# Attention backward loop: the block-end statistics spread over GpSimd, VectorE and several units, with dK and dV taken in other units

## The chip, the cores and the metric

The kernel runs on one core of one Trainium2 chip. The metric is the device time of one launch in microseconds (us); several launches are taken and the median is given. Engines: PE is TensorE (PEld its weight loads), DVE is VectorE, ACT is ScalarE, POOL is GpSimd, SP is SyncE, which here issues the DMAs. Where runs of two kernels are compared, the ratio is the mean time of one kernel's runs over that of the other's of the same rounds, so it is not quite the ratio of the medians that stand beside it. The experiments ran on two chips of the same kind (e4, e6, e7 and e9 on one, the others on another, by the record); each was measured beside the kernel before on its own chip, so runs of different rounds are compared by their ratios.

## The reference, cut to what matters

The program computes a forward pass and all gradients of two attention blocks. Only block B's backward matters here: 16 query heads that share one key and one value head, sequence 2048, head size 28.

```python
q = (x @ wq).reshape(B, S, H, Dh)          # 16 heads
k = x @ wk;  v = x @ wv                    # one head each
scores = einsum("bhqd,bkd->bhqk", q, k) * Dh**-0.5
p = softmax(scores);  o = einsum("bhqk,bkd->bhqd", p, v)
...                                        # o @ wo, then jax.vjp for all gradients
```

The kernel recomputes p tile by tile. With e = exp(score), row sum l, D = sum(dO*o) and dS = p*(dP - D), it needs dV = p^T dO, dK = dS^T q, dQ = dS k. The kernel puts 1/l and D into the small operand: the tile `don` holds dO/l in its columns and D/l in column 0, so that dP - D, already divided by l, falls out of one matmul. Other names below: `dsT` is dS with keys on the partitions, `dsx` is dsT transposed on DVE for dK, `eN` is e transposed by a DMA for dV, `doT` is `don` transposed for dP, `onat` is the normalised o, and `qX` holds the queries that dK reads. The granted clock is the share of full speed at which TensorE was allowed to run.

## The kernel before

The loop walks through 64 blocks (256 queries x 2 heads) of eight units (256 keys each). It is software-pipelined: in the program's unit u, block b's exp is made for u = 8b to 8b+7, its statistics follow at 8b+9, its dP and dS 16 units after the exp, its dQ 18 units after it, its dK later still. So every unit holds work of several blocks. I call the units 0 to 7 by u mod 8. The order of the code is the order on each engine.

```python
for u in range(NU + 26):
    w = u - 16
    sp = two score banks (of three, shared);  dp = two dP banks (of two)
    rows_SD(u, sp, dp)                                   # PE: scores of u, dP of u-16
    nc.scalar.activation(out=et[..0..], in_=sp[0], func=Exp)              # ACT, L671
    nc.vector.tensor_tensor(out=dst[:, 0], in0=dp[0], in1=e.., op=mult)   # DVE, L676: dsT
    nc.scalar.activation(out=cp, in_=dp[1], func=Copy)                    # ACT, L678
    nc.gpsimd.tensor_tensor(out=dst[:, 1], in0=cp, in1=e.., op=mult)      # POOL, L679: dsT
    nc.scalar.activation(out=et[..1..], in_=sp[1], func=Exp)              # ACT, L681
    if u % 2 == 1: nc.sync.dma_start_transpose(en, et)   # SP: eN, for dV
    # [...]
    e = u - 9                                            # unit 1: the chain
    if e >= 0 and e % 8 == 0 and e // 8 < NB:
        onp = psS.tile(..., name="sps")                  # PE transposes of o into a score bank
        nc.vector.reciprocal(out=r_, in_=onp[..0:1])                      # L701
        nc.vector.tensor_tensor(out=onv, in0=onp, in1=r_, op=mult)        # L705: onat
        nc.vector.tensor_tensor(out=dn, in0=dnv, in1=r_, op=mult)         # L709: don
        nc.gpsimd.tensor_tensor(out=prod, in0=dnv, in1=onv, op=mult)      # L711
        nc.vector.tensor_reduce(out=Dq, in_=prod, op=add)                 # L713
        nc.vector.tensor_tensor(out=dn[..0:1], in0=Dq, in1=r_, op=mult)   # L714
    e = u - 13                                           # unit 5: don transposed, copied to doT
    x = u - 26                                           # dK: two groups of four matmuls in each unit
    # [...] all of them need dsx of the whole block
    # PE: o of u-1 and dQ of u-18, both into the bank oq
    # dV: in every second unit, from u = 8b + 14 on, one group of four matmuls; needs eN and don
    # unit 0: DVE copies o (oTs);  unit 1: ACT copies dQ (L774)
    nc.vector.transpose(out=dsx[b][:, tp], in_=dsT[u - 18])               # DVE, L780
```

## Time and profile before

1722.71 us, median of 3 runs (1716.72 to 1724.99). I took each unit's length from the trace as the time from the start of its first exp (L671) to that of the next unit, median over the blocks (here and in the later tables from block 4 on):

| unit | 0 | 1 | 2 | 3 | 4 | 5 | 6 | 7 | block |
|---|---|---|---|---|---|---|---|---|---|
| before, us | 1.46 | 2.02 | 4.51 | 2.11 | 1.74 | 1.51 | 1.46 | 1.52 | 15.68 |

Units 0 and 5 to 7 take about 1.5 us; units 1 to 4 take longer. (The unit medians add up to more than the block's 15.68, since the blocks differ: about every third takes 16.6 us.) From the page of the kernel before, the span in 40 slices: busy tenths of PE and ACT, and the granted clock of PE. The loop fills slices 14 to 37, the last of them in part.

```profile
PE   2786767992985988888888888888888988888398
ACT  0321200120449887787778778778778777875122
PEclk9996886995985598888888888888888888888699
```

No engine is full, and the clock is at eight tenths. The engine that the stall holds up shows in the list of waits (who waited for whom, us in total, times, longest):

```profile
ACT eT L671 <- PE dps L623: 174.5, 100, 2.9
DVE dsT L676 <- PE dps L623: 156.8, 265, 3.6
PE dk_acc L623 <- DVE dsx L780: 120.8, 64, 2.6
```

Once in each of 64 blocks PE waits for DVE's dsx, and ACT and DVE then wait for PE. The timeline of DVE through units 1 and 2 of one block (start us, length us, engine, line, what; in brackets idle time before it and what ended it) shows why dsx is late:

```profile
1008.67 0.64 DVE L676 TENSOR_TENSOR dsT<-dps,eT 128x512 bf16<-128x512 f32 x1
1009.24 0.16 DVE L701 RECIPROCAL rl<-sps 128x4 f32<-128x4 f32 x1
1009.43 0.29 DVE L705 TENSOR_TENSOR onat<-sps,rl 128x128 bf16<-128x128 f32 x1
1009.64 0.99 DVE L709 TENSOR_TENSOR don<-do_nat,rl 128x128 bf16<-128x128 bf16 x1
1010.95 0.29 DVE L713 TENSOR_REDUCE Dq<-prod 128x4 f32<-128x128 f32 x1 [0.32 <-POOL prod L711]
1011.27 0.18 DVE L714 TENSOR_TENSOR don<-Dq,rl 128x4 bf16<-128x4 f32 x1
1011.35 0.70 DVE L780 STREAM_TRANSPOSE dsx<-dsT 128x512 f32<-128x512 f32 x1
1011.98 0.65 DVE L676 TENSOR_TENSOR dsT<-dps,eT 128x512 bf16<-128x512 f32 x1
```

Between the dsT of unit 1 and the transpose that completes dsx lie 2.1 us of chain. The timelines of PE and of ACT at the same place have the consequence:

```profile
1012.11 1.04 PE L623 MATMUL dk_acc<-dsx,qX 32*32 32x512 bf16 x8 [1.93 <-DVE dsx L780]
```

```profile
1014.69 0.60 ACT L671 ACTIVATE eT<-sps 128x512 bf16<-128x512 f32 x1 [2.94 <-PE dps L623]
```

After the gap the eight dK matmuls take 1.04 us; in a warm unit they take 0.61. In the clock records a low stretch (half speed) of 3.4 or 6.8 us begins once a block, during such a gap or within 1.6 us of its end: 60 stretches, 273 us, between block 4 and the end of the loop. The longest PE gap of a block is 1.93 us (median).

### The profile page before, as it was taken

Reading aid. Unit: us, or ns where it says so; the run is one execution under the profiler, and the core shown is the slowest. Engines: PE = TensorE matmul, PEld = TensorE weight load, DVE = VectorE, ACT = ScalarE, POOL = GpSimd, SP = SyncE. Lnnn points to the kernel's source line nnn. Section 1 sums busy time; section 2 is a strip of 40 time slices with the busy share of each in tenths; the row PEclk is TensorE's granted clock in tenths of the full one; section 3 lists DMA queues with packets and bytes.
Section 4 is the critical chain, followed back from the end, with each engine's and each line's share of the span. In section 5 each row is a group of like instructions: output and inputs, shape, how many; then the busy total and the mean of one; then the engine's idle time right before and its main releaser. Section 6 shows DMA issues by size and latency. Waiting matters only on the chain. (4 is left out here: it accounts for less than half of the span.)

```text
span 1718.1 us, 40732 instructions
## 1 busy us (share of the span) xinstructions
PE 1394.5 (81%) x16282; PEld 511.1 (30%) x16282; DVE 1065.9 (62%) x2113; ACT 986.5 (57%) x1907; POOL 658.5 (38%) x632
## 2 busy tenths in 40 slices
PE   2786767992985988888888888888888988888398
PEld 1234345541331222222222222222222222222153
DVE  1866578401131487787788777788777778778120
ACT  0321200120449887787778778778778777875122
POOL 3000000001300365565566556566556556656100
PEclk9996886995985598888888888888888888888699
DMA  9000300018110987987987977978878978884611
GB/s 117 1 1 30 99 4 4 17 45 175 44 42 0 160 137 137 154 143 139 155 139 143 148 136 142 149 136 149 150 132 153 145 131 158 144 131 83 155 54 54
DMA packets 628542, 181.96 MB, mean 106 GB/s; under 512 B 593456, under 2 KB 624144, under 8 KB 628352
## 3 DMA queue, kind: packets, MB, share of 16 engines
q1 hardware_dynamic: 628048, 178.91, 58.8%
q8 instruction: 127, 2.08, 0.5%
q0 software_dynamic: 304, 0.45, 0.3%
q14 instruction: 63, 0.52, 0.1%
HBM read 24.81 MB, written 13.99 MB: 23 GB/s over the span
## 5 line engine op out<-in xcount | busy, mean ns | idle before, releaser
L679 POOL TENSOR_TENSOR dsT<-cp,eT 128x512 bf16<-128x512 bf16 x512 | 590.6, 1154 | 405.6 <-ACT cp L678 345.0
L623 PE MATMUL dk_acc<-dsx,qX 32*32 32x512 bf16 x4096 | 369.9, 441 | 120.8 <-DVE dsx L780 120.8
L676 DVE TENSOR_TENSOR dsT<-dps,eT 128x512 bf16<-128x512 f32 x512 | 347.8, 679 | 165.9 <-PE dps L623 156.8
L671 ACT ACTIVATE eT<-sps 128x512 bf16<-128x512 f32 x512 | 307.2, 600 | 206.7 <-PE dps L623 174.5
L780 DVE STREAM_TRANSPOSE dsx<-dsT 128x512 f32<-128x512 f32 x512 | 357.9, 699 | 1.0
L678 ACT ACTIVATE cp<-dps 128x512 bf16<-128x512 f32 x512 | 304.6, 595 | 15.8 <-PE dps L623 15.8
L681 ACT ACTIVATE eT<-sps 128x512 bf16<-128x512 f32 x512 | 310.5, 606 | 0.0
L623 PE MATMUL dps<-doT,vT_rep 32*128 32x256 bf16 x2048 | 258.9, 300 | 2.1 <-DVE dsT L676 1.5
L623 PE MATMUL oq<-eT,vaug 128*32 128x256 bf16 x2048 | 229.8, 310 | 0.0
L623 PE MATMUL oq<-dsT,kn 128*32 128x256 bf16 x2048 | 226.7, 306 | 0.0
L623 PEld LDWEIGHTS <-kT_rep 32*128 32x128 bf16 x2048 | 85.7, 94 | 208.0 <-issue 188.8
L623 PEld LDWEIGHTS <-vaug 128*32 128x32 bf16 x2048 | 60.4, 97 | 270.5 <-issue 270.2
L623 PEld LDWEIGHTS <-qX 32*32 32x32 bf16 x4096 | 67.8, 92 | 230.3 <-issue 219.0
L623 PE MATMUL dv_acc<-eN,don 128*32 128x512 bf16 x1024 | 115.7, 434 | 0.0
L159 POOL MEMSET woB_pr_3208<- 128x448 bf16 x1 | 0.5, 475 | 281.9 <-DMA out_dram<-gx_sb 281.9
L623 PEld LDWEIGHTS <-vT_rep 32*128 32x128 bf16 x2048 | 78.9, 94 | 8.6 <-issue 8.0
L623 PE MATMUL sps<-qT_B_3185,kT_rep 32*128 32x256 bf16 x512 | 67.2, 314 | 11.4 <-ACT qT_B_3188 L600 9.0
L489 ACT CAST gw_sb<-gw_acc 128x448 bf16<-128x448 f32 (+1 forms) x12 | 6.4, 531 | 111.3 <-PE gw_acc L94 111.3
L623 PE MATMUL sps<-qT_B_3186,kT_rep 32*128 32x256 bf16 x512 | 67.0, 311 | 0.7 <-ACT eT L681 0.3
L623 PE MATMUL sps<-qT_B_3187,kT_rep 32*128 32x256 bf16 x512 | 64.3, 301 | 0.5
L623 PE MATMUL sps<-qT_B_3188,kT_rep 32*128 32x256 bf16 x512 | 64.2, 301 | 0.6
L623 PEld LDWEIGHTS <-kn 128*32 128x32 bf16 x2048 | 60.2, 97 | 8.5 <-issue 8.5
(557 smaller groups left out, 1732.5 us busy)
## 6 DMA issues: line engine op xcount, KB each, us to landing
qX<-qn_d SPq DMA_DIRECT2D x128, 64.0 KB
eN<-eT SPq DMA_TRANSPOSE x256
xb_nat<-in_B_x_dram SPq DMA_DIRECT2D x2, 1792.0 KB
qn_d<-qn_sb SPq DMA_DIRECT2D x16, 128.0 KB
on_d<-onat SPq DMA_DIRECT2D x8, 256.0 KB
onat_B<-on_d SPq DMA_DIRECT2D x1, 2048.0 KB
xa_nat<-in_A_x_dram SPq DMA_DIRECT2D x1, 1792.0 KB
out_dram<-out_a_sb SPq DMA_DIRECT2D x16, 112.0 KB
```

Source lines behind the costliest of these rows:

```text
L159: nc.gpsimd.memset(t[:], 0.0)
L489: nc.any.tensor_copy(out=gsb[0:rows], in_=acc[0:rows, :].rearrange("p (h c) -> p h c", c=32)[:, :, 1:1 + DH])
L623: nc.tensor.matmul(out, lhsT=lhsT, rhs=rhs, start=start, stop=stop, tile_position=pos, skip_group_check=True)
L671: nc.scalar.activation(out=et[:, u % 2, 0, :], in_=sp[0][:, :], func=ACT.Exp, scale=scale)
L676: nc.vector.tensor_tensor(out=dst[:, 0, :], in0=dp[0][:, :], in1=ew[:, w % 2, 0, :], op=ALU.mult)
L678: nc.scalar.activation(out=cp[:, :], in_=dp[1][:, :], func=ACT.Copy)
L679: nc.gpsimd.tensor_tensor(out=dst[:, 1, :], in0=cp[:, :], in1=ew[:, w % 2, 1, :], op=ALU.mult)
L681: nc.scalar.activation(out=et[:, u % 2, 1, :], in_=sp[1][:, :], func=ACT.Exp, scale=scale)
L780: nc.vector.transpose(out=dsx[b][:, tp, :, :, :].rearrange("p h t c -> p (h t c)").bitcast(F32), in_=dsT[y][:, :, :].rearrange("p h c -> p ...
```

## The change

The intent is to take the chain's long tail off DVE in unit 1, to give dK two units more until its dsx is needed, and to keep dK and dV out of each other's units. The diff, cut:

```diff
-                for u in range(NU + 26):
+                for u in range(NU + 28):
 # [...] e = u - 9: reciprocal and onat stay on DVE
-                        nc.vector.tensor_tensor(out=dn[:], in0=dnv, in1=r_..., op=ALU.mult)
-                        nc.gpsimd.tensor_tensor(out=prod[:], in0=dnv, in1=onv, op=ALU.mult)
-                        nc.vector.tensor_reduce(out=Dq[:, :, :, 0], in_=prod[:], axis=AX.X, op=ALU.add)
-                        nc.vector.tensor_tensor(out=dn[:, :, :, 0:1], in0=Dq[:], in1=r_[:], op=ALU.mult)
+                        nc.gpsimd.tensor_tensor(out=dn[:], in0=dnv, in1=r_..., op=ALU.mult)
-                    e = u - 13
+                    e = u - 10
+                        nc.gpsimd.tensor_tensor(out=prod[b][:], in0=do_nat[...], in1=onat[qc][...], op=ALU.mult)
+                    e = u - 12
+                        nc.vector.tensor_reduce(out=Dq[:, :, :, 0], in_=prod[b][:], axis=AX.X, op=ALU.add)
+                        nc.gpsimd.tensor_tensor(out=don[b][:, :, :, 0:1], in0=Dq[:], in1=rl[b][:], op=ALU.mult)
+                    e = u - 14
 # [...] transposes of don, doT
-                    x = u - 26
-                    if 0 <= x and x // 8 < NB:
-                        for m in (2 * (x % 8), 2 * (x % 8) + 1):
+                    x = u - 28
+                    if 0 <= x and x // 8 < NB and x % 8 < 6:
+                        m0 = 3 * (x % 8) - max(0, x % 8 - 4)
+                        for m in range(m0, m0 + (3 if x % 8 < 4 else 2)):
 # [...]
-                    if u >= 14 and (u - 14) % 2 == 0:
-                        b, i = divmod((u - 14) // 2, 4)      # dV: one group in every second unit
+                    if u >= 18 and u % 8 in (2, 3) and (u - 18) // 8 < NB:
+                        b, h = divmod(u - 18, 8)             # dV: two groups in units 2 and 3
+                        for qb in range(2):
```

So dK has three groups in units 4 to 7 and two in units 0 and 1; dV has two groups in units 2 and 3. The last unit that reads a block's dsx is the same as before.

## The prediction

> **What bounds it now.** The attention loop runs from 557 to 1565 us (timeline): 64 blocks of eight units. The start-to-start times of the first exp of each unit repeat in every block: units 4 to 8 take 1.46 to 1.75 us, unit 1 takes 2.02, unit 2 takes 4.51 (median), unit 3 takes 2.1. A block is 15.7 us (15.9 on average once both halves of the loop run).
> An undisturbed unit is bound by ACT: its three 128x512 activations start every 0.485 us (1.46 us), though each shows as 0.60. With 0.56 us for the copy of dQ in unit 1, ACT alone needs 12.2 us a block. PE at full clock needs nearly as much: I read 0.44 us for scores and dP, 0.54 for two groups of dK, 0.33 for o and dQ, 0.2 for one group of dV, about 11.7 us a block.
> The excess of 3.5 us sits in one place. In unit 1 DVE runs the statistics chain: reciprocal, onat, don (0.99 us, though 0.28 where GpSimd is idle), a 0.35 us wait for GpSimd's product, reduction 0.29, 0.18. Only then, 2.0 us late, comes the transpose that completes dsx, and dK's first matmul in unit 2 needs the whole block's dsx: the list of waits has 64 waits of PE for dsx, 120.8 us, and ACT then waits 174.5 us for dP. After it the granted clock falls to one half, once a block, 273 us between 600 and 1560; that makes units 3 and 4 slow. The Trainium skill ("TensorE: Matmul & The Clock Gate", Part 1) says that an idle window gates the clock to half until about 3.4 us of activity; the trace agrees: low stretches of 3.4 and 6.8 us.
>
> **What the change does.** DVE keeps 0.45 us of the chain in unit 1; the reduction (0.29) comes three units later, its input ready. GpSimd gains don (estimate 0.47 us, from the product of the same size, 0.473) and a tiny product (estimate 0.2). It idles about 0.3 us a unit, so they fit; dsT is needed two units later. dK starts in unit 4, two units after its dsx is complete, so the 120.8 us wait should vanish, and with it the cooling. dV moves to units 2 and 3. PE's work is the same, but units 4 to 7 now carry three groups of dK each; I allow 0.1 us for each.
>
> **Sum.** Units: 1.46 + 2.02 + 2x1.5 + 4x1.56, doT 0.1: 12.7 us a block, against 15.9. For 62 blocks 787 us against 986: 199 us saved. The two further units of drain cost about 2. Predicted 1525 us, range 1492 to 1575; below 1492 would be under ACT's 12.2. Chances: faster 0.96, within 2% 0.03, slower 0.01.
>
> **What would show it.** PE's wait for dsx nearly gone; unit 2 about 1.5 us; PE clock near 1.0 through the loop; ACT busy nearly throughout it; don on GpSimd near 0.47 us; DVE's busy time down by about 60 us; the rest of the program unchanged.
>
> **What would make it wrong.** DMA: transposes of e take 2.5 to 2.65 us each when queued back to back (first blocks) and four a block are needed, 10.6 of 12.7 us plus the loads of qX; if others slow them the loop ends at 13 or more. A remaining stall in unit 1 or 2 (score buffers, oTs) that still cools PE once a block: 13.3 us, 1565. Three-group units that cost 1.8: 13.7. GpSimd's don slow under DVE traffic, delaying dsT.

## The result, and the profile after

1524.14 us (median of 4 runs, 1519.44 to 1537.1) against 1720.11 us (4 runs) before. The ratio is 0.8871, with a 95% interval of 0.8811 to 0.8931. The outputs are correct.

| unit | 0 | 1 | 2 | 3 | 4 | 5 | 6 | 7 | block |
|---|---|---|---|---|---|---|---|---|---|
| before, us | 1.46 | 2.02 | 4.51 | 2.11 | 1.74 | 1.51 | 1.46 | 1.52 | 15.68 |
| after, us | 1.46 | 2.03 | 1.46 | 1.52 | 1.46 | 1.55 | 1.81 | 1.51 | 12.78 |

The same three rows of the page after; the loop now fills slices 15 to 37, the first and the last in part:

```profile
PE   1796777799479769999999999999999999998389
ACT  0340220021034599999999999999999999994022
PEclk9997788799779756999999999999999999999599
```

From slice 16 to 36 PE and ACT are busy nine tenths or more (a 9 is 90% or more); the clock is so from slice 17 on, after two low stretches that end at 587 and 601 us. The list of waits after, same three waits:

```profile
DVE dsT L676 <- PE dps L623: 37.2, 158, 2.1
ACT eT L671 <- PE dps L623: 15.1, 62, 0.7
PE dk_acc L623 <- DVE dsx L792: 0.4, 1, 0.4
```

DVE at the same place, units 1 and 2 of one block:

```profile
981.23 0.65 DVE L676 TENSOR_TENSOR dsT<-dps,eT 128x512 bf16<-128x512 f32 x1
981.80 0.16 DVE L701 RECIPROCAL rl<-sps 128x4 f32<-128x4 f32 x1
982.00 0.29 DVE L705 TENSOR_TENSOR onat<-sps,rl 128x128 bf16<-128x128 f32 x1
982.20 0.70 DVE L792 STREAM_TRANSPOSE dsx<-dsT 128x512 f32<-128x512 f32 x1
982.83 0.65 DVE L676 TENSOR_TENSOR dsT<-dps,eT 128x512 bf16<-128x512 f32 x1
```

The transpose follows 0.97 us after the dsT of unit 1 starts, where it was 2.68. The windows view (length, then busy us and instructions of each engine, granted clock, DMA share, GB/s) cut at the first and last exp shows where the time went; first before, then after:

```profile
557.50:1563.30 1005.80, 873.32 (x13171) 271.65 (x13172) 782.34 (x1429) 797.67 (x1580) 597.27 (x558) 0.84 0.84 144
1563.30:1718.10 154.80, 113.18 (x997) 52.25 (x996) 42.42 (x94) 39.43 (x82) 24.61 (x26) 0.86 0.33 81
```

```profile
561.80:1374.20 812.40, 786.40 (x13163) 288.99 (x13166) 713.85 (x1303) 790.19 (x1578) 626.43 (x684) 0.98 1.08 178
1374.20:1522.80 148.60, 110.02 (x1004) 52.20 (x1004) 40.22 (x92) 39.41 (x81) 24.84 (x28) 0.87 0.35 84
```

The loop took 193.4 us less, the rest after it 6.2 less (4.8 of these in the drain, from the last exp to the last dK matmul: 34.2 before, 29.4 after), and the part ahead of it, which the change doesn't touch, was 4.3 us longer in this one execution. ACT's work stayed (798 and 790 us), and it now fills 97% of the loop. PE fills as much of it (786 of 812 us), so the busy shares alone do not tell which of the two bounds the loop.

### The profile page after: what moved, and what is told of

It is laid out like the page before. It is cut to its first block, busy times and chain, and to the rows that moved or that the text cites. A ratio compares the mean times of both kernels' runs of the same rounds, so it can differ in the third digit from the quotient of the medians.

```text
span 1522.8 us, 40668 instructions
## 1 busy us (share of the span) xinstructions
PE 1309.8 (86%) x16282; PEld 530.7 (35%) x16282; DVE 996.5 (65%) x1985; ACT 978.8 (64%) x1907; POOL 687.9 (45%) x760
## 5 line engine op out<-in xcount | busy, mean ns | idle before, releaser
L623 PE MATMUL dk_acc<-dsx,qX 32*32 32x512 bf16 x4096 | 289.6, 377 | 0.4 <-DVE dsx L792 0.4
L623 PE MATMUL dps<-doT,vT_rep 32*128 32x256 bf16 x2048 | 262.0, 273 | 7.4 <-ACT cp L678 0.4
L623 PE MATMUL oq<-eT,vaug 128*32 128x256 bf16 x2048 | 218.2, 283 | 0.5
L623 PE MATMUL oq<-dsT,kn 128*32 128x256 bf16 x2048 | 203.6, 279 | 0.3 <-ACT qT_B_3188 L786 0.2
L623 PEld LDWEIGHTS <-kT_rep 32*128 32x128 bf16 x2048 | 90.4, 91 | 195.3 <-issue 156.8
L623 PEld LDWEIGHTS <-vaug 128*32 128x32 bf16 x2048 | 68.2, 94 | 189.2 <-issue 188.8
L623 PEld LDWEIGHTS <-vT_rep 32*128 32x128 bf16 x2048 | 85.5, 91 | 20.6 <-issue 19.8
L623 PE MATMUL dv_acc<-eN,don 128*32 128x512 bf16 x1024 | 86.3, 385 | 0.0
L623 PE MATMUL sps<-qT_B_3185,kT_rep 32*128 32x256 bf16 x512 | 65.7, 291 | 11.6 <-ACT qT_B_3188 L600 9.0
L623 PE MATMUL sps<-qT_B_3186,kT_rep 32*128 32x256 bf16 x512 | 64.9, 282 | 0.9 <-ACT eT L681 0.2
L623 PE MATMUL sps<-qT_B_3188,kT_rep 32*128 32x256 bf16 x512 | 62.3, 276 | 0.8
L623 PE MATMUL sps<-qT_B_3187,kT_rep 32*128 32x256 bf16 x512 | 62.1, 276 | 0.8
```

The lines of the kernel that those rows point to most:

```text
L623: nc.tensor.matmul(out, lhsT=lhsT, rhs=rhs, start=start, stop=stop, tile_position=pos, skip_group_check=True)
```

## The experiments

All of them change lines of that loop alone. The table has every run's unit times, as above; the text takes them one by one.

| run | 0 | 1 | 2 | 3 | 4 | 5 | 6 | 7 | block | median us | ratio to before (95%) |
|---|---|---|---|---|---|---|---|---|---|---|---|
| before | 1.46 | 2.02 | 4.51 | 2.11 | 1.74 | 1.51 | 1.46 | 1.52 | 15.68 | 1720.11 | 1 |
| after | 1.46 | 2.03 | 1.46 | 1.52 | 1.46 | 1.55 | 1.81 | 1.51 | 12.78 | 1524.14 | 0.8871 (0.8811 to 0.8931) |
| e1_dk_only | 1.46 | 2.03 | 2.82 | 1.51 | 2.01 | 1.93 | 1.46 | 1.55 | 15.13 | 1671.38 | 0.9702 (0.9683 to 0.9721) |
| e2_chain_only | 1.46 | 2.02 | 1.74 | 1.51 | 1.46 | 1.52 | 1.84 | 1.51 | 13.04 | 1562.18 | 0.9063 (0.9031 to 0.9096) |
| e3_don_dve | 1.46 | 2.02 | 2.03 | 1.51 | 1.46 | 1.55 | 1.81 | 1.51 | 13.33 | 1558.73 | 0.9043 (0.9026 to 0.9061) |
| e5_pool_unspread | 1.46 | 2.02 | 4.26 | 1.99 | 1.71 | 1.62 | 1.46 | 1.52 | 15.50 | 1686.87 | 0.9783 (0.9765 to 0.9801) |
| e4_dv_even | 1.46 | 2.02 | 1.46 | 1.52 | 1.67 | 1.51 | 2.05 | 1.51 | 13.18 | 1567.95 | 0.9114 (0.9080 to 0.9148) |
| e13_qx_spread | 1.46 | 2.02 | 1.46 | 1.52 | 1.67 | 1.51 | 2.05 | 1.51 | 13.18 | 1557.65 | 0.9026 (0.9000 to 0.9051) |
| e6_oq_spare (wrong) | 1.46 | 2.40 | 1.46 | 1.52 | 1.46 | 1.55 | 1.75 | 1.51 | 13.04 | 1541.32 | 0.8968 (0.8937 to 0.9000) |
| e7_dq_dve | 1.46 | 2.03 | 1.71 | 1.51 | 1.46 | 1.55 | 1.81 | 1.51 | 13.07 | 1538.79 | 0.8953 (0.8924 to 0.8981) |
| e9_comb (wrong) | 1.46 | 1.72 | 3.35 | 1.99 | 1.76 | 1.53 | 2.55 | 1.51 | 15.90 | 1689.21 | 0.9820 (0.9777 to 0.9862) |
| e10_rebalance | 1.46 | 2.02 | 1.46 | 1.52 | 1.46 | 1.55 | 1.59 | 1.51 | 12.56 | 1515.42 | 0.8780 (0.8751 to 0.8808) |
| e11_move_dq | 1.46 | 1.55 | 1.91 | 1.51 | 1.46 | 1.55 | 1.46 | 1.72 | 12.67 | 1516.88 | 0.8792 (0.8768 to 0.8816) |
| e12_move_dq2 | 1.46 | 1.55 | 2.02 | 1.51 | 1.46 | 1.55 | 1.46 | 1.56 | 12.63 | 1512.36 | 0.8780 (0.8746 to 0.8815) |

### The later dK, with the dV that goes with it: e1_dk_only

The kernel before with the change's hunks for dK, dV and the loop's length; the chain as it was.

```diff
-                    x = u - 26                                  # two groups in each unit
+                    x = u - 28                                  # 3, 3, 3, 3, 2, 2 groups, as in the change
-                    if u >= 14 and (u - 14) % 2 == 0:           # dV
+                    if u >= 18 and u % 8 in (2, 3) and (u - 18) // 8 < NB:
```

> Kernel before, but dK two units later in six of eight units and dV in the other two, as the change has it; the statistics chain stays undivided on DVE. Theory (the chain's hold on DVE delays the next dsT as well as dsx, so dK's wait is only one of two costs): PE no longer waits for dsx, but unit 2 is still held by the late dsT of DVE: about 1.4 us above the changed kernel's 12.8 us a block, 14.2, or 15 if PE still cools: 1610 to 1660 us. Rival (dK's wait for dsx is the whole cost): 12.8 us a block, 1525 us.

It is only 3% faster, 1671 us. The wait of dK for dsx is gone (0.4 us in all), as the rival needs, but the gain did not follow. The timelines of DVE and of PE show that the wait moved to the next thing that the chain delays; DVE first:

```profile
1066.40 1.02 DVE L709 TENSOR_TENSOR don<-do_nat,rl 128x128 bf16<-128x128 bf16 x1
1067.74 0.28 DVE L713 TENSOR_REDUCE Dq<-prod 128x4 f32<-128x128 f32 x1 [0.32 <-POOL prod L711]
1068.06 0.18 DVE L714 TENSOR_TENSOR don<-Dq,rl 128x4 bf16<-128x4 f32 x1
1068.14 0.70 DVE L780 STREAM_TRANSPOSE dsx<-dsT 128x512 f32<-128x512 f32 x1
1068.77 0.65 DVE L676 TENSOR_TENSOR dsT<-dps,eT 128x512 bf16<-128x512 f32 x1
```

```profile
1069.48 0.26 PE L623 MATMUL dps<-doT,vT_rep 32*128 32x256 bf16 x1 [1.10 <-DVE dsT L676]
```

PE's next dP goes into the bank that the dsT of unit 2 reads, and that dsT stands behind the whole chain. The list of waits of this run has it as a wait of its own, one in each block:

```profile
PE dps L623 <- DVE dsT L676: 69.6, 63, 2.0
```

In the kernel before this wait was hidden behind the longer one for dsx. After the gap of 1.10 us the clock is still low in most blocks: 50 stretches of half speed, 171 us, from block 4 to the end of the loop. The theory holds in kind; the total lies 11 us above its range.

### The spread chain alone: e2_chain_only

The changed kernel with the hunks for dK, dV and the loop's length taken back (the reverse of the edit above).

> Changed kernel, but dK and dV taken as in the kernel before (dK from the first unit after dsx is complete, two groups in each unit). Theory (the time that DVE is held is the root; with it short, dsx is complete at about the time PE gets there): PE waits some 0.2 us a block for dsx, unit 2 near 1.8 us, no cooling, block 12.8 to 13.2 us, 1525 to 1550 us. Rival (the later dK is what pays): dK still waits, PE still cools, block above 15 us, over 1660 us.

It is 9.4% faster than before, most of the change's 11.3%, with dK as early as it ever was. PE's wait for dsx fell from 120.8 to 14.2 us in all, 0.2 a block; unit 2 takes 1.74 us; only three low stretches of the clock remain, 10 us. So the time that the chain holds DVE is the root, and the later dK and dV together are a smaller second part. The sum of the two parts alone, 3.0 and 9.4%, is 1.1 points more than both together: each takes away a piece of the same unit-2 stall.

The run was 12 us above its range, and the block median (13.04) accounts for only 62 x 0.26 = 16 of the 38 us to the changed kernel. Most of the rest (18 us) lies in seven blocks, numbers 9, 17, 25 and so on to 57, in which unit 6 took 3.1 to 5.1 us. I had not predicted these; the list of waits has a new line:

```profile
PE dv_acc L623 <- DMA eN<-eT: 12.3, 8, 2.8
```

### dV as before, and the loads that stand in its way: e4_dv_even, e13_qx_spread

e4_dv_even is the changed kernel with dV's hunk alone taken back:

```diff
-                    if u >= 18 and u % 8 in (2, 3) and (u - 18) // 8 < NB:
+                    if u >= 14 and (u - 14) % 2 == 0:    # one group in every second unit, as before
```

> Changed kernel with dV taken as before: from six units after the block's first exp, one group in every second unit, so that dK and dV meet in one unit. Theory 1 (dV's later start also pays: in the blocks that load qX the transposes of e land late, and an earlier dV waits for them): seven stalls of 2 to 3 us in the blocks with a load of qX, and 0.2 us a block because units 4 and 6 now hold four groups: 1545 to 1560 us. Rival (when dV is taken does not matter): within 0.5% of the changed kernel, 1525 us, no block over 13.2 us.

It came out at 1568 us, 8 above the range. Three things show. Units 4 and 6 now hold three groups of dK and one of dV: 1.67 and 2.05 us instead of 1.46 and 1.81, 0.4 us a block, 25 us in all. Again seven blocks, about eight apart, are long (14.7 to 18.5 us); in six of them PE waits for eN in unit 6 (1.2 to 3.5 us), and in the seventh, block 16, it doesn't: a low stretch of the clock makes its unit 4 slow, and why is open. And e4_dv_even differs from e2_chain_only in the later dK alone, yet is no faster (0.9114 against 0.9063, other rounds, intervals that overlap; block 13.18 against 13.04). With dV early, the later dK by itself gains nothing: what it frees in unit 2 it loses in the units that it shares with dV. PE in the last dV matmul of the first group, from its timeline:

```profile
1007.84 0.48 PE L623 MATMUL dv_acc<-eN,don 128*32 128x512 bf16 x1 [2.80 <-DMA eN<-eT]
```

The queue of SP shortly before that, from its timeline:

```profile
980.64 2.95 SPq L684 DMA_TRANSPOSE eN<-eT  x1
983.64 8.83 SPq L660 DMA_DIRECT2D qX<-qn_d  x16
992.58 1.96 SPq L684 DMA_TRANSPOSE eN<-eT  x1
```

Every eight blocks sixteen loads of qX go through the one queue that issues the transposes of e; for 9 us no transpose is issued, and four a block are needed. In the packets, each transpose then takes 2.3 to 3.5 us and the next starts at once, until the queue has caught up some two blocks later. To test that it is these loads, e13_qx_spread is e4_dv_even with the loads one per unit:

```diff
-                    if u % 64 == 0 and hasS:
-                        # [...] for a in range(4): for B in range(4): nc.sync.dma_start(qx[...])
+                    if u % 64 < 16 and hasS:
+                        a, B = divmod(u % 64, 4)     # qX allocated at u % 64 == 0
+                        # [...] one nc.sync.dma_start(qX[qc][...])
```

> As the run with dV in every second unit, but the sixteen loads of qX are issued one in each of sixteen units instead of all in one. Theory (in that run seven blocks are 1.5 to 5.4 us long because the sixteen loads stand ahead of the transposes of e in the one issuing queue, for 9 us, and dV waits for eN): no block over 13.6 us, total 15 to 20 us less, about 1550 us. Rival (the long blocks come from something else at that point of the loop): still seven long blocks, 1568 us.

The seven long blocks are gone (from block 4 on none is over 13.8 us; I had said 13.6), and the list of waits has 0.9 us for eN in place of 11.2. The run is 10 us faster by the medians, 0.9026 against 0.9114; I expected 15 to 20. So the later dV of the change pays in two ways: it keeps four groups out of one unit, and it gives eN four units more to land. In the changed kernel PE never waited for eN.

### don back on DVE: e3_don_dve

```diff
-                        nc.gpsimd.tensor_tensor(out=dn[:], in0=dnv, in1=r_..., op=ALU.mult)
+                        nc.vector.tensor_tensor(out=dn[:], in0=dnv, in1=r_..., op=ALU.mult)
```

> Changed kernel with one edit: the product that makes don goes back from GpSimd to DVE, in unit 1. Theory: it takes about 1.0 us there because GpSimd is busy[...] (0.28 alone), so the dsT of unit 2 is 0.8 to 1.0 us late and unit 2 takes about 2.1 us: block 13.4, 1560 us. Rival (spreading and the later dK are enough, the engine does not matter): within 1% of the changed kernel, 1525 us.

1559 us, as the theory said: unit 2 takes 2.03 us, nothing else moved. This one instruction costs 1.9% (0.9043 over 0.8871, runs of different rounds). From the tile view of don, its minimum, median and maximum in ns on DVE in this run, and on POOL in the changed kernel:

```profile
L709 DVE TENSOR_TENSOR don<-do_nat,rl x64: 280/990/1272, 572.3 to 1410.6; 128x128 bf16<-128x128 bf16 x64
```

```profile
L709 POOL TENSOR_TENSOR don<-do_nat,rl x64: 396/402/406, 573.2 to 1378.8; 128x128 bf16<-128x128 bf16 x64
```

The Trainium skill ("GPSIMD Engine Reference", section 1) says that GpSimd shares its SBUF interfaces with VectorE and that a DVE instruction with two SBUF inputs contends with it; its section 4.1 advises VectorE for elementwise work, as GpSimd is about twice as slow with two inputs. The trace agrees with the first: in the kernel before, don ran on DVE from 1009.64 to 1010.63 while GpSimd's dsT ran from 1009.33 to 1010.48, so it ended only after that. It is so in all 61 of the 64 blocks, in both runs, in which don started during a dsT of GpSimd: it ended 0.14 to 0.15 us after the dsT. In the other three it started first and took 0.28. The advice is reversed here: 0.40 us on GpSimd, in its turn, against 0.99 on DVE in the middle of GpSimd's work, though DVE needs 0.28 when it starts first.

### GpSimd without the spreading: e5_pool_unspread

The kernel before, with don (after the product) and the last product on GpSimd, all in unit 1:

```diff
-                        nc.vector.tensor_tensor(out=dn[:], in0=dnv, in1=r_..., op=ALU.mult)
                         nc.gpsimd.tensor_tensor(out=prod[:], in0=dnv, in1=onv, op=ALU.mult)
+                        nc.gpsimd.tensor_tensor(out=dn[:], in0=dnv, in1=r_..., op=ALU.mult)
                         nc.vector.tensor_reduce(out=Dq..., in_=prod[:], ...)
-                        nc.vector.tensor_tensor(out=dn[:, :, :, 0:1], in0=Dq[:], in1=r_[:], op=ALU.mult)
+                        nc.gpsimd.tensor_tensor(out=dn[:, :, :, 0:1], in0=Dq[:], in1=r_[:], op=ALU.mult)
```

> Kernel before, but don and the last small product go to GpSimd, all still in unit 1, dK and dV as before. Theory (it is the wait of the DVE for a product behind GpSimd's dsT, not the work, that holds it): the reduction still waits for the product, the transpose that completes dsx comes only about 0.15 us earlier than in the kernel before, block about 15.4 us, 1700 us. Rival (relieving DVE of the work of don is what pays): half of the gain or more, below 1620 us.

1687 us, 2.2% faster: clear of the noise, but with an interval that reaches below 2%, so that the verdict at 2% is "unclear". PE's wait for dsx is still 104.9 us in 64 waits, and DVE's wait for the product grew from 22.6 to 75.4 us. Taking work off DVE does little while DVE still waits, in the same unit, for a product that stands behind GpSimd's 1.15 us dsT. The dsx transpose starts 2.44 us after the dsT of unit 1, against 2.68 before. Moving the reduction to a unit where its input is ready is what frees DVE: with it, e2_chain_only gained 9.4%.

### What holds the changed kernel: e6_oq_spare, e7_dq_dve, e9_comb

In the changed kernel unit 6 takes 1.81 us and unit 1 takes 2.03. e6_oq_spare puts the transposes' results into the unused half of the bank oq:

```diff
-                        onp = psS.tile([P, 2, 2, 32], F32, name="sps")
+                        onp = oq[:, 256:384].rearrange("p (q h c) -> p q h c", q=2, h=2)
-                        tp2 = psS.tile([P, 1024], BF16, name="sps")
+                        tp2 = oq[:, 384:512].bitcast(BF16)
```

> Changed kernel; the results of the two transposes of the chain go to the unused half of the bank that holds o and dQ, not to a score buffer. Unit 6 takes 1.81 us in the changed kernel. Theory (there PE is the limit: 12 matmuls of dK and the transposes follow each other without a gap; only a wait of 0.12 us for the score buffer goes away): unit 6 near 1.70, block 12.65, 1515 to 1520 us. Rival (the shared score buffer costs the 0.3 us): unit 6 near 1.5, 1505 us. Both: unit 1 stays at 2.02, where ACT is busy throughout.

The result was wrong (relative error 1.24), and it was slower than the changed kernel: PE's o and dQ matmuls now waited 43.1 us for onat, so unit 1 took 2.40. This was my mistake. The Trainium skill ("PSUM — Partial Sum Buffer", "The four PSUM rules") says that a matmul which starts an accumulation clears the written-bits of the whole bank in the groups of 32 partitions that it writes, so that a running sum in the same bank is overwritten by its next matmul. o and dQ accumulate in that bank over 16 matmuls each. The wrong result fits that rule; no run isolates it. Its unit 6 (1.75) fits the theory, but a wrong kernel that waits elsewhere settles nothing.

e7_dq_dve moves the copy of dQ from ACT to DVE:

```diff
-                        nc.scalar.activation(out=qT_B[g][...], in_=oq[64:128, 0:256], func=ACT.Copy, scale=scale)
+                        nc.vector.tensor_scalar(out=qT_B[g][...], in0=oq[64:128, 0:256], scalar1=scale,
+                                                scalar2=None, op0=ALU.mult)
```

> Changed kernel; the copy of dQ out of PSUM (0.38 us) moves from ACT to DVE. Theory (in unit 1 two things end at the same time: ACT's copy, and the score buffer that the chain's transpose holds until onat is read): unit 1 stays at 2.0, and the dsT of unit 2 comes 0.4 us later on DVE, so unit 2 takes about 1.7: block 13.0, 1535 us. Rival (ACT alone bounds unit 1): unit 1 takes 1.5, block 12.3, 1495 us.

It is slower than the changed kernel, 1539 us, as the theory said: unit 1 stays at 2.03, since the scores of unit 2 still need the bank that onat is being read from, and ACT, freed of the copy, sits idle there for 0.44 us; DVE's dsT is later. e9_comb joined both edits with two more:

```diff
 # [...] both edits above, and
-                    e = u - 9  /  e = u - 10  /  e = u - 12
+                    e = u - 10 /  e = u - 11  /  e = u - 13
-                        # dK groups 3, 3, 3, 3, 2, 2
+                        # dK groups 3, 3, 2, 3, 3, 2
```

> Three edits on the changed kernel together: transposes to the spare half as above, the copy of dQ on DVE, and the normalisation (reciprocal, onat, don, product, reduction) one unit later so that it does not meet that copy on DVE; dK spread 3, 3, 2, 3, 3, 2 groups over its six units, two where the transpose is. Theory (PE, ACT and DVE each need 11.5 to 11.7 us a block and no unit has a longest wait): every unit 1.46 to 1.55, block 11.9, 1470 to 1480 us. Rival (something that the changed kernel's 12.8 hides comes next, such as the transposes of e, 10.6 us a block plus qX): no better than 12.4, over 1500 us.

It inherits the wrong result (error 1.23) and the shared bank, for which PE waited 92.6 us for onat. The transposes of don waited another 64.1 us for GpSimd's last small product, which is issued too late for them when it moves one unit. It took 1689 us with these waits and 32 low stretches of the clock, and says nothing about its theory.

### Better balanced: e10_rebalance, e11_move_dq, e12_move_dq2

e10_rebalance changes the numbers of dK's groups only:

```diff
-                        m0 = 3 * (x % 8) - max(0, x % 8 - 4)
-                        for m in range(m0, m0 + (3 if x % 8 < 4 else 2)):
+                        m0 = (0, 3, 6, 8, 11, 14)[x % 8]
+                        for m in range(m0, m0 + (3, 3, 2, 3, 3, 2)[x % 8]):
```

> Changed kernel, but dK's 16 groups spread 3, 3, 2, 3, 3, 2 instead of 3, 3, 3, 3, 2, 2, so that the unit with the transposes of don has two groups. Theory (unit 6 takes 1.81 us because PE has 12 matmuls of dK and the two transposes there): unit 6 falls to about 1.55 and no other unit rises by more than 0.1, block 12.5 to 12.6, 1508 to 1515 us. Rival (unit 6 is held by the score buffer that the transposes use or by DVE's copy of doT): unit 6 stays at 1.8, 1524 us.

The median of 1515 us is at the upper end of the range. Unit 6 fell from 1.81 to 1.59 and no other unit rose: PE's own work, three groups of dK plus the transposes of don, had filled it. This settles what e6 could not. The ratio to before is 0.8780, about 1% below that of the changed kernel, and the intervals just fail to overlap, but the two were not run in the same rounds; the unit times carry the claim.

e11_move_dq frees ACT from the dQ copy and moves the rest of the chain out of DVE's way, with the score banks as in the changed kernel (the edit is shortened here, in part to words):

```diff
-                    e = u - 9  /  e = u - 10  /  e = u - 12  /  e = u - 14
+                    e = u - 10 /  e = u - 11  /  e = u - 13  /  e = u - 15
-                        # dK groups 3, 3, 3, 3, 2, 2; ACT copies dQ; copies of o and dQ ahead of DVE's dsx
+                        # dK groups 3, 3, 3, 2, 2, 3; DVE copies dQ; copies of o and dQ after DVE's dsx
```

> Changed kernel with the copy of dQ on DVE and what that needs: on DVE the transpose of dsx goes ahead of the copies of o and dQ, the normalisation (reciprocal, onat, don, product) moves one unit later, out of the unit of the dQ copy, the reduction and the transposes of don one unit later too, dK spread 3, 3, 3, 2, 2, 3; score buffers as in the changed kernel. Theory (ACT's 12.2 us a block is the floor of the changed kernel, and with the copy gone 11.7 is; DVE needs 11.6): unit 1 near 1.5, block 12.0 to 12.2, 1475 to 1490 us. Rival (with DVE as full as ACT the delays only move): block 12.6 or more, over 1510 us.

e12_move_dq2 differs from it in two lines:

```diff
-                        # dK groups 3, 3, 3, 2, 2, 3
+                        # dK groups 3, 3, 3, 1, 3, 3
```

> As the run that moved the copy of dQ to DVE, but dK spread 3, 3, 3, 1, 3, 3, with one group in the unit of don's transposes. Theory (that unit, 1.72 us, is full on PE): it falls to 1.5, unit 2 stays at 1.9 because the score buffer waits for onat: block 12.35 to 12.45, 1500 to 1507 us. Rival (DVE holds that unit): it stays at 1.7, 1517 us.

In both, unit 1 fell from 2.03 to 1.55 as meant, and unit 2 rose from 1.46 to 1.91 and 2.02: the bank that onat holds and DVE's later dsT meet there (in e11_move_dq ACT waits 21.6 us for scores, in the changed kernel 2.3). e12_move_dq2 did bring unit 7 from 1.72 to 1.56, so that unit too was full on PE, but its total missed the range by 5 us. At 0.8792 and 0.8780 they are no better than e10_rebalance, which needs two changed lines. The rival of e11_move_dq had the result right: the delay moved. That DVE's fullness is the whole reason is argued, not shown. PE also begins to wait for eN again at this pace (1.3, 0.8 and 2.3 us in the three runs; one block of e12_move_dq2 took 17.1).

## Why the prediction was right

**The total.** 1525 predicted, 1524.14 measured. Part of that agreement is luck: the loop saved 193.4 us where I said 199, the drain was 4.8 us shorter where I said 2 longer (it too had held a block end with its stall), and the untouched part ahead of the loop was 4.3 us longer in the profiled run.

**What bounds it.** No run with the copy of dQ on ACT went below ACT's 12.2 us a block (e10_rebalance came nearest, with 12.56), and the loop's ACT is now busy 97%. But ACT is not alone: e7_dq_dve shows that unit 1 stays at 2.03 without the copy, because the scores wait for onat's bank too. Unit 2 came to 1.46 us (1.5 predicted), the clock in the loop from block 4 on had no low stretch at all, and DVE's busy time fell by 69 us (60 predicted). don on GpSimd took 0.40 us (0.47), the small product 0.22 (0.2).

**"I allow 0.1 us for each" of the three-group units.** The sum for units 4 to 7 was right (6.34 predicted, 6.33 measured: 1.46 + 1.55 + 1.81 + 1.51), its distribution was not. Units 4, 5 and 7, with three groups too, stayed at 1.46 to 1.55; unit 6, where the transposes of don join them, cost 0.3. e10_rebalance shows it by taking one group away there.

**"The excess of 3.5 us sits in one place."** This step was incomplete. The text put the stall down to dK's wait for dsx and let the two later units of dK make it vanish. e1_dk_only shows that those (with dV moved as well) take the wait away and bring a quarter of the gain (3.0 of 11.3%), because the dsT of unit 2 stands behind the same chain on DVE and PE waits for that instead. e2_chain_only shows that a short chain alone brings 9.4%. The prediction held because the change does both. How much of the gain is the waits and how much the low clock that follows them (273 us before, none after), no run separates.

**What the prediction did not say.** It named the transposes of e as a risk to the new pace, but did not see that the later dV is what takes that risk away. e2_chain_only, e4_dv_even and e13_qx_spread show that at the faster pace the earlier dV would have waited for eN in every eighth block. The slow kernel before had hidden this: its blocks left the queue time to catch up, and no wait for eN stands in its list.

## What to carry to other kernels

When an in-order engine holds a long chain, ask for everything that stands behind it on that engine, not only for the wait that the profile lists: the longest wait hides the next one. Split such a chain at its waits on another engine and put each piece in a unit where its input is already there; moving the work to the other engine without that brought 2% here (e5_pool_unspread), with it 9.4% (e2_chain_only), and 11.3% with dK and dV moved too. A faster pace uncovers slow transfers that the old pace had hidden, so give the consumer of a queued DMA its slack before the stall is taken away.

## What the Trainium skill lacked or had wrong

- "TensorE: Matmul & The Clock Gate" ("HAM oscillation") words its rule as no PE-idle gaps over about 3.4 us. Here gaps far shorter lowered the clock: a largest gap of 1.93 us per block (before) and of 1.68 (e5_pool_unspread) gave 60 low stretches in 60 blocks, 1.10 us (e1_dk_only) gave 50, and 0.63 us (e3_don_dve) gave none. No threshold follows: ten of e1_dk_only's gaps of 1.1 us, and four single gaps of 0.9 to 1.3 us in e2_chain_only, lowered nothing. Low stretches of 3.4 us and twice that do agree with its window. The traces show a grid besides: within a run, all low stretches of the loop start at whole multiples of 3.41 us from each other. In the step of that grid before each low stretch PE was busy for 42 to 63% (before) and 64 to 70% (e1_dk_only) by the profile's modelled ends, and in e3_don_dve no step was under 79%. So the idle share of such a step fits better than the length of one gap, though no sharp limit came out (e2_chain_only has a step of 61% with no low stretch after it, and the stretch in block 16 of e4_dv_even follows one of 87%). The section after that one on the same page does tell of short idles that make the clock oscillate; it is the short rule that is too loose.
- "GPSIMD Engine Reference" (section 4.1) compares the engines each by itself. It lacks what contention does to the choice (that the two engines block each other is told on another page, "SBUF — State Buffer"): the same 128x128 product took 0.28 us on DVE when it started first, 0.99 on DVE when GpSimd's product was already running, and 0.40 on GpSimd.
- "DMA: Bandwidth & Descriptors" has no figure for what a burst of plain loads does to transposes in the same issuing queue. Here sixteen loads of 64 KB held the queue of SP for 8.8 us, and dV waited up to 3.5 us for a transpose behind them (e4_dv_even).
